# A two-filter FFT mix on one core: a read-back in halves, two row loads apart, a gate turned by four wide matmuls, and a reordered program

## The chip, the core and the metric

The kernel runs on one core of a Trainium2 chip. TensorE (PE; its weight loads are shown as PEld), VectorE (DVE), ScalarE (ACT) and GpSimd (POOL) each work through their own list of instructions in order; SyncE (SP) issues nearly all DMA transfers, also in order. The metric is device microseconds (us) for one launch; the profile gives in addition the span from the first to the last instruction of one execution.

## The reference

For x of 2048 x 1024 (bf16) the kernel computes

```
g = sigmoid((x * gate_w).sum(-1))          # one number per row of 1024
a = irfft2(rfft2(x) * (A_w_r + i A_w_i))   # filter A
b = irfft2(rfft2(x) * (B_w_r + i B_w_i))   # filter B
out = g * a + (1 - g) * b
```

with both inverse transforms rounded to bf16. B_x is not used.

## The kernel before, in words

The two-dimensional transforms are matmuls with constant tables. A row number is written s1 + 16 * s2; s2 (128 values) lies on the partitions, s1 (16 values) beside it. Columns are split by symmetry into an even ("e", 0) and an odd ("o", 1) part. The work has these stages, and each has a short name in the program's order:

- **x, W, c**: loads by SP of rows of x, of the 16 weight blocks W:0 to W:15 (512 KB each; 0 to 7 into `Ro`, 8 to 11 into `wx`, 12 to 15 into `y`), and of constants (F1, EZ, E, w0, FD, WF, PM, WJ, IG).
- **F1:s1:part:bank** (line 330): transform over s2, eight matmuls into a PSUM bank. There are eight banks, 0 to 7. **FC** copies half of the bank into one of eight temporary slots in `wx`, **FD** (DVE, line 378) forms sum and difference into `y`; or **FX** copies the whole bank and **FP** does the same on POOL.
- **F2:n:half:bank** (line 454), for 16 units n (0 to 7 even, 8 to 15 odd): transform over columns; **T** copies it out. **F3:n** (line 484) finishes the forward transform over s1; **X** copies.
- **P:n** (DVE, line 501): product with both filters, 4096 elements per partition. For the even units **Y, NA, N** mend the first column.
- **J:n** (line 547): inverse over s1, into two pairs of banks; **R:n:half:engine** (lines 200 or 202) copies each pair into a buffer `rl` (five buffers). **H:n:half** (line 559) stores it to a scratch array in DRAM; **L:part:v** (line 564) reads it back in another arrangement, eight reads v of 512 KB for each part, after all eight units of that part are stored. The even part goes into `Re`, the odd into `Ro`.
- **V:part:v:s:bank** (line 575): inverse over s2, with the gate folded into the tables EA = g * E and EB = (1 - g) * E; **VC** copies. **C** or **U** (lines 600 and 591): inverse over columns. Even results: **E**, **ES** and **EF**, or **EX** and **EQ**, leave them in `Re`. Odd results are added to and subtracted from them: **OR** and **QD** on DVE, **OC**, **OP** and **QP** for POOL. **S:S:v** stores the output.
- Gate: **gc** makes coefficients on POOL, **GH** contracts y with them on TensorE, **GC** copies to `zs`, **GT:g** turns the result by small matmuls (line 417), **GK** copies, **GZ** and **GS** make the sigmoid, **GA** and **GB** build EA and EB for four s1 at a time.

A token such as `R:15:0:A` names the operation, its unit or row, and the engine (A, D, P, S). One string `ORDER` lists all 575 tokens, written out by hand; each engine takes its own in that order, and semaphores are set where data, a PSUM bank or a buffer is shared. No planner orders anything when the kernel is built. The products that follow the odd read-back alternate with V's on TensorE, and each V must be copied out before its U or C.

Of the kernel before, what the change touches and what calls it, by code (L numbers as in the profile page):

```python
# [10 lines left out]
P = 128  # L11
# [25 lines left out]
F2:7:0:3 F2:5:1:0 Y:3:4 P:3:b Y:2:1 NA:3:D T:5:0:A T:5:1:A F3:4:6 X:4:A c:S:FD:1:2 GT:2:5 F2:7:1:2 GK:D NA:2:D N:2:D T:7:0:D
J:0:0:4 N:3:D T:7:1:A R:0:1:A R:0:0:D J:3:2:6 GZ:0:0 R:3:1:D R:3:0:A F3:5:4 GS:0 c:S:IG X:5:A F2:6:0:7 P:4:b J:2:0:2 Y:4:6
T:6:0:A R:2:1:A F2:6:1:7 NA:4:D GZ:1:5 T:6:1:A R:2:0:D N:4:D GS:1 F3:7:2 Y:5:4 X:7:A P:5:b F2:8:1:5 F3:6:6 W:S:9 NA:5:D H:1:1
H:1:0 N:5:D H:0:1 H:0:0 H:2:0 T:8:1:A H:3:1 W:S:14 J:4:2:0 W:S:15 X:6:A F2:8:0:4 R:4:0:A H:2:1 T:8:0:A F2:9:1:5 R:4:1:A H:3:0  # L40
J:5:2:6 R:5:0:A Y:7:0 P:7:b H:5:0 F2:9:0:1 Y:6:4 P:6:b F3:8:2 R:5:1:A NA:7:D NA:6:D N:7:D T:9:1:D T:9:0:D X:8:A GA:D:0 N:6:D
F2:10:1:0 F2:10:0:4 H:4:1 T:10:1:A T:10:0:A GB:D:0 P:8:b F3:9:2 X:9:A J:7:6:0 J:6:2:4 R:7:1:A F3:10:0 R:7:0:A F2:11:0:6
R:6:1:A GA:D:8 R:6:0:D H:5:1 H:4:0 H:7:1 H:7:0 H:6:0 H:6:1 W:S:13 F2:12:0:3 X:10:A F2:11:1:7 F2:12:1:0 T:11:0:A W:S:12
T:11:1:A F2:14:1:1 F3:11:6 P:9:b T:12:0:A L:0:0 J:8:4:2 T:12:1:A X:11:A T:14:1:A R:8:0:A P:10:b GA:D:4 R:8:1:D F2:13:1:0
F3:12:6 T:13:1:A F2:13:0:1 F2:14:0:0 X:12:A T:13:0:D GA:D:12 J:9:2:4 P:11:b R:9:1:D T:14:0:A L:0:2 J:10:0:6 L:0:1 R:9:0:A
L:0:6 L:0:7 L:0:4 L:0:5 V:0:0:1:2 F2:15:1:3 R:10:0:A F3:14:0 R:10:1:A VC:0:0:1:A J:11:4:6 X:14:A F2:15:0:0 R:11:1:A C:0:0:1:1
H:8:1 P:12:b H:8:0 H:9:1 H:9:0 H:10:0 H:10:1 V:0:0:0:6 R:11:0:A T:15:1:D GB:D:4 T:15:0:D P:14:b F3:13:2 V:0:1:1:7 EX:0:1:A
VC:0:0:0:A X:13:A J:12:0:4 VC:0:1:1:A R:12:1:A F3:15:2 X:15:A EQ:0:1:0:P V:0:2:1:6 R:12:0:D C:0:0:0:5 EX:0:0:A C:0:1:1:7
V:0:2:0:2 EX:1:1:A VC:0:2:0:A J:14:0:4 P:13:b VC:0:2:1:A R:14:0:A J:13:6:2 C:0:2:1:0 R:14:1:A R:13:0:A V:0:1:0:4 P:15:b
EX:2:1:D GB:D:12 EQ:2:1:0:D R:13:1:D VC:0:1:0:A C:0:2:0:5 EX:2:0:A H:12:1 H:12:0 J:15:0:6 H:11:0 H:11:1 R:15:1:A V:0:6:0:4  # L50
V:0:6:1:5 H:14:0 R:15:0:A H:14:1 C:0:1:0:3 H:13:0 H:13:1 GB:D:8 EX:1:0:A VC:0:6:0:A EQ:1:1:1:D EQ:2:0:0:D H:15:1 V:0:4:1:6
V:0:5:1:7 V:0:5:0:2 H:15:0 VC:0:6:1:D V:0:4:0:0 C:0:6:0:4 EQ:2:0:1:P EQ:1:0:1:P VC:0:5:0:D C:0:6:1:3 L:0:3 V:0:7:0:5 L:1:1
VC:0:5:1:A L:1:3 E:6:0:A L:1:6 L:1:7 C:0:5:1:7 L:1:0 EQ:0:0:1:P VC:0:4:1:A EQ:0:0:0:P C:0:5:0:1 VC:0:7:0:D V:0:7:1:2
C:0:4:1:4 ES:5:1:A VC:0:4:0:A EF:5:1 EQ:1:1:0:P EQ:0:1:1:P ES:5:0:A L:1:2 L:1:5 E:6:1:D EF:5:0 ES:4:1:D VC:0:7:1:A C:0:4:0:6
V:0:3:1:0 C:0:7:1:2 EQ:2:1:1:P EQ:1:0:0:D VC:0:3:1:A EX:7:1:A V:0:3:0:5 C:0:7:0:3 C:0:3:1:7 VC:0:3:0:A ES:4:0:A V:1:1:0:0
V:1:1:1:2 C:0:3:0:1 EX:7:0:D EF:4:1 EF:4:0 VC:1:1:0:A V:1:3:1:4 E:3:0:A U:1:1:0:3 V:1:3:0:1 E:3:1:D EQ:7:0:1:P VC:1:3:1:A
C:1:3:1:7 OC:1:0:A VC:1:1:1:D EQ:7:1:0:D VC:1:3:0:A QD:3:1:0 V:1:6:1:5 C:1:3:0:4 QD:3:0:0 U:1:1:1:2 V:1:6:0:6 VC:1:6:1:A
V:1:0:0:1 QD:3:1:1 VC:1:6:0:A EQ:7:0:0:P V:1:0:1:5 OP:1:0:1 VC:1:0:0:A QD:3:0:1 OP:1:0:0 C:1:6:1:0 OR:1:1:1 OR:1:1:0 QD:6:1:0
U:1:0:0:7 VC:1:0:1:A QP:3:0:1:P C:1:6:0:2 QD:6:0:0 V:1:5:1:1 V:1:2:1:4 U:1:0:1:3 L:1:4 QD:6:0:1 OC:0:0:A V:1:5:0:5 QD:6:1:1
VC:1:2:1:A VC:1:5:1:A QP:3:1:0:P QP:3:1:1:P QP:3:0:0:P U:1:2:1:6 VC:1:5:0:A OR:0:1:1 OP:0:0:1 OR:0:1:0 OR:2:1:0 OR:2:1:1  # L60
# [35 lines left out]
def make_constants():  # L96
# [24 lines left out]
    c["EZ"] = _bf16np(EZ.reshape(128, 128) / 128)  # L121
    j = np.arange(256) - 255.5
# [60 lines left out]
def gated_mix(ctx, tc, x_in, we_in, wo_in, w0_in, gw_in, out):  # L183
# [97 lines left out]
    def gate_coef(e):  # L281
# [3 lines left out]
        q.memset(C["one"][:], 1.0)  # L285
# [67 lines left out]

    def f1_ps(s1, par):

        if ("F1", s1, par) in PS:
            return PS["F1", s1, par].rearrange("p (a b) -> p a b", a=2)
        return PS["F1", s1, "b"].rearrange("p (a b) -> p a b", a=2)[:, :, sl(par)]
# [38 lines left out]
    def gate_hat(k):  # L397
        ps = PS["gh"] = ptile(k)
        for v in range(2):
            for e in range(2):  # L400
                for b in range(2):
                    for j in range(4):
                        nc.tensor.matmul(ps[32 * j:32 * j + 32, 0:512], lhsT=C["gwz"][:, v, e, b, :],  # L403
                                         rhs=y[:, v, e, b, 8 * j:8 * j + 8, :, :].rearrange("p t s c -> p (t s c)"),
                                         start=(v + e + b == 0), stop=(v + e + b == 3))

    def gate_copy(e):
        zs = TM["zs"] = C["EB"][:].rearrange("p a b -> p (a b)")[:, 0:512].rearrange("p (s f) -> p s f", s=NS1)
# [49 lines left out]
    def f2c(n, tt, e):  # L458
# [3 lines left out]
        cp(e, Ts[n][:, tt], PS.pop(("T", n, tt)))  # L462

# [91 lines left out]

    def scratch_store(n, tt, q="S"):
# [26 lines left out]

    def i3(par, v, s, k):
# [8 lines left out]
    def i3f(par, v, s, k):  # L593
# [3 lines left out]
        for ch in range(4):  # L597
            o = (ch // 2) * 256
            g = C["IG"][:, par, ch % 2]
            nc.tensor.matmul(ps[:, o:o + 256], lhsT=Vs[par, v][:, s, ch, :], rhs=g[:, o:o + 256], start=(ch % 2 == 0), stop=(ch % 2 == 1))  # L600

# [121 lines left out]
```

## Time and profile before

| | us |
|---|---|
| median of 3 runs | 116.35 (114.51 to 118.43) |
| profiled execution | 115.38 |
| its span | 113.6 |
| PE, DVE, ACT, POOL busy | 99.9, 97.7, 87.1, 41.0 |
| DMA | 36.79 MB, mean 324 GB/s |
| store of the last scratch half, to landing | 3.42 |
| 16 weight products on DVE (line 501) | 2.28 each |

Busy times are of the one profiled execution. A share over the whole span mixes stages, so stages are read from stretches of time. In timelines and in the chain, the columns are start, length, engine, line, operation, tiles and count; brackets hold the idle time just before and what ended it. "DMA sc<-rl" is a scratch store, "re<-sc" and "ro<-sc" are the read-backs of the even and the odd part. SPq is SP's own queue of DMA issues. Where a time of one token is given, it is the instruction of that place in its engine's list.

### The profile page before, as it was taken

Reading aid. Unit: us, or ns where it says so; the run is one execution under the profiler, and the core shown is the slowest. Engines: PE = TensorE matmul, PEld = TensorE weight load, DVE = VectorE, ACT = ScalarE, POOL = GpSimd, SP = SyncE. Lnnn points to the kernel's source line nnn. Section 1 sums busy time; section 2 is a strip of 40 time slices with the busy share of each in tenths; the row PEclk is TensorE's granted clock in tenths of the full one; section 3 lists DMA queues with packets and bytes.
Section 4 is the critical chain, followed back from the end, with each engine's and each line's share of the span. In section 5 each row is a group of like instructions: output and inputs, shape, how many; then the busy total and the mean of one; then the engine's idle time right before and its main releaser. Section 6 shows DMA issues by size and latency. Waiting matters only on the chain.

```text
span 113.6 us, 3933 instructions
## 1 busy us (share of the span) xinstructions
PE 99.9 (88%) x1616; PEld 69.7 (61%) x1619; DVE 97.7 (86%) x157; ACT 87.1 (77%) x142; POOL 41.0 (36%) x61
## 2 busy tenths in 40 slices
PE   5999979999988879798998989979999699999910
PEld 2699969776564455554654556556988477767400
DVE  0079989999998999999999999999559849999870
ACT  4267848999989999999999999999976565635200
POOL 1089999100000000000000008002590469999970
PEclk9999999999999999999999999999999999999995
DMA  3999999999999919995899999998968999445984
GB/s 85 352 325 396 398 395 406 401 404 409 400 415 391 330 68 256 292 372 208 281 298 414 414 398 349 378 388 282 309 197 338 351 408 362 190 188 226 371 326 185
DMA packets 17794, 36.79 MB, mean 324 GB/s; under 512 B 1904, under 2 KB 10736, under 8 KB 17776
## 3 DMA queue, kind: packets, MB, share of 16 engines
q1 hardware_dynamic: 17488, 36.44, 87.6%
q8 instruction: 12, 0.20, 0.7%
q10 hardware_dynamic: 288, 0.10, 0.4%
q14 instruction: 6, 0.05, 0.1%
HBM read 23.96 MB, written 12.58 MB: 322 GB/s over the span
## 4 chain that ended last, share of the span: by engine, by line
DMA 43%; PE 36%; DVE 5%; issue 4%; ACT 4%; SPq 3%; DVEq 1%; ACTq 0%
DMA sc<-rl 17%; DMA re<-in_x_dram 12%; PE ps L591 8%; PE ps L575 6%; PE ps L454 6%; DMA re<-sc 5%; DMA ro<-sc 5%; PE ps L330 4%; PE ps L547 4%; DMA y<-in_wo_dram 3%; ACT rl L200 3%; PE ps L484 3%; PE ps L600 2%; PE ps L403 2%; SPq L559 2%
## 5 line engine op out<-in xcount | busy, mean ns | idle before, releaser
L625 POOL TENSOR_TENSOR re<-wx 128x256 f32<-128x256 f32 x11 | 9.5, 888 | 60.2 <-DMA re<-sc 48.4
L200 ACT COPY wx<-ps 128x256 f32<-128x256 f32 (+1 forms) x42 | 18.3, 476 | 8.3 <-PE ps L330 5.2
L200 ACT CAST rl<-ps 128x1024 bf16<-128x1024 f32 x24 | 23.6, 1036 | 0.9 <-PE ps L547 0.5
L200 ACT CAST V<-ps 128x512 bf16<-128x512 f32 x27 | 15.7, 613 | 7.8 <-PE ps L575 5.1
L454 PE MATMUL ps<-fd,y 128*128 128x256 bf16 x128 | 17.6, 273 | 2.3 <-ACT ea L430 0.6
L501 DVE TENSOR_TENSOR p<-X,ro 128x4096 bf16<-128x4096 bf16 x8 | 18.1, 2279 | 0.0
L547 PE MATMUL ps<-p,wj 32*64 32x512 bf16 x512 | 17.1, 380 | 0.9 <-ACT V L200 0.4
L200 ACT CAST X<-ps 128x1024 bf16<-128x1024 f32 x16 | 17.0, 1060 | 0.6 <-PE ps L417 0.3
L378 DVE TENSOR_TENSOR y<-ps,wx 128x256 bf16<-128x256 f32 x48 | 16.4, 411 | 0.4 <-ACT wx L200 0.4
L330 PE MATMUL ps<-f,re 128*128 128x128 bf16 x256 | 15.2, 220 | 0.7 <-DMA re<-in_x_dram 0.7
L330 PEld LDWEIGHTS <-re 128*128 128x128 bf16 x256 | 14.7, 99 | 1.6 <-DMA re<-in_x_dram 0.9
L454 PEld LDWEIGHTS <-y 128*128 128x128 bf16 x128 | 11.4, 97 | 6.6 <-issue 5.2
L200 ACT CAST T<-ps 128x512 bf16<-128x512 f32 x26 | 15.0, 625 | 0.4 <-PE ps L484 0.2
L378 POOL TENSOR_TENSOR y<-wx 128x256 bf16<-128x256 f32 x16 | 11.1, 734 | 5.2 <-ACT wx L200 5.2
L547 PEld LDWEIGHTS <-wj 32*64 32x64 bf16 x512 | 7.6, 103 | 7.1 <-issue 3.2
L645 DVE TENSOR_TENSOR ot<-re,ps 128x512 bf16<-128x512 f32 x18 | 11.3, 682 | 0.6 <-POOL re L625 0.5
L591 PE MATMUL ps<-ig,V 128*128 128x512 bf16 x45 | 11.5, 379 | 0.2
L600 PE MATMUL ps<-ig,V 128*128 128x256 bf16 x80 | 11.2, 272 | 0.2 <-ACT rl L200 0.2
L484 PE MATMUL ps<-T,wf 64*64 64x512 bf16 (+1 forms) x128 | 10.3, 334 | 0.9 <-issue 0.3
L202 DVE CAST rl<-ps 128x1024 bf16<-128x1024 f32 x8 | 9.7, 1218 | 0.4 <-PE ps L547 0.4
L657 POOL TENSOR_TENSOR ot<-pq 128x512 bf16<-128x512 f32 x8 | 9.9, 1276 | 0.0
L575 PEld LDWEIGHTS <-ro 128*128 128x128 bf16 x128 | 7.8, 98 | 2.9 <-DMA ro<-sc 1.4
(62 smaller groups left out, 143.8 us busy)
## 6 DMA issues: line engine op xcount, KB each, us to landing
sc<-rl SPq DMA_DIRECT2D x32, 256.0 KB, 4.7
ro<-in_we_dram SPq DMA_DIRECT2D x8, 512.0 KB, 7.9
re<-sc SPq DMA_DIRECT2D x8, 512.0 KB, 7.9
ro<-sc SPq DMA_DIRECT2D x8, 512.0 KB, 6.9
re<-in_x_dram SPq DMA_DIRECT2D x7, 512.0 KB, 7.7
out_dram<-ot SPq DMA_DIRECT2D x7, 512.0 KB, 2.6
wx<-in_wo_dram SPq DMA_DIRECT2D x4, 512.0 KB, 9.6
y<-in_wo_dram SPq DMA_DIRECT2D x4, 512.0 KB, 4.9
```

The source lines that it names most:

```text
L200: nc.scalar.copy(out=out, in_=in_)
L330: nc.tensor.matmul(o, lhsT=lh, rhs=rh, start=(h == 0), stop=(h == 1))
L378: Q[e].tensor_tensor(yo[:, v, k:k + n, s1, :], a.rearrange("p (k c) -> p k c", c=4), b.rearrange("p (k c) -> p k c", c=4), op)
L454: nc.tensor.matmul(ps[:, v * 256:v * 256 + 256], lhsT=y[:, v, par, b, 2 * t:2 * t + 2, :, :].rearrange("p j s c -> p (j s c)"), rhs=C["FD" ...
L484: nc.tensor.matmul(view(ps[ho, tt * 512:(tt + 1) * 512], dst), lhsT=lh, rhs=view(T[hp(jh), tt, :], src), start=(w == 0), stop=(w == 1))
L501: nc.vector.tensor_tensor(p[:], xb, wb, ALU.mult)
L547: nc.tensor.matmul(o, lhsT=lh, rhs=src[r, ri, wi, tt], start=(q == 0), stop=(q == 3))
L575: nc.tensor.matmul(ps[:, ch * 128:ch * 128 + 128], lhsT=RR[par][:, v, ch // 2, s, c0 + 256 * ab:c0 + 256 * ab + 128], rhs=Ew[:, s1, :], st ...
L591: nc.tensor.matmul(ps, lhsT=Vs[par, v][:, s, ch, :], rhs=rh, start=(ch == 0), stop=(ch == 3))
L600: nc.tensor.matmul(ps[:, o:o + 256], lhsT=Vs[par, v][:, s, ch, :], rhs=g[:, o:o + 256], start=(ch % 2 == 0), stop=(ch % 2 == 1))
L645: nc.vector.tensor_tensor(otile(v)[:, s, h, :], EV[:, v, s], PS["O", 1, v, s], (ALU.add, ALU.subtract)[h])
L657: Q[e].tensor_tensor(otile(v)[:, :, h, 256 * g:256 * g + 256], t[:, :, 0], t[:, :, 1], (ALU.add, ALU.subtract)[g])
```

## The change

Five things change.

- The load of rows 2 and 3 of x becomes two loads.
- The read-back L:1:1 (the first of the odd part) becomes L:1:1:0 and L:1:1:1, each with the rows of one s.
- GT (four tokens, 64 matmuls of one column) becomes one token Gt of four matmuls with 128 rows, 128 columns of weights and four columns of data. For it GH reads y in another order of the same elements, GC writes `zs` in another arrangement, and gc sets a mask of four columns by five memsets instead of one.
- Tokens change places. On SP, w0 and E go behind x:14, WJ:0:4 and PM come earlier, FD:1:2 and WJ:4:16 too; the order of the weights becomes 1, 2, 0, 3, 5, 7, 11, 4, 10, 8, 6, 9, 15, 12, 14, 13 (before 0, 2, 1, 5, 3, 7, 6, 10, 4, 8, 11, 9, 14, 15, 13, 12); H:8:0 goes ahead of L:0:0, H:2:0 behind H:5:0. Many PSUM banks are renumbered.
- Copies change engines. To ScalarE: FC:1:e, T:15:0, VC:0:6:1, VC:0:5:0, VC:0:7:0, VC:1:1:1, VC:1:4:1, ES:4:1, EX:7:0. To VectorE: FC:3:e, VC:0:1:1, R:15:0, EX:1:0, E:6:0, VC:0:4:1, EX:7:1, OC:1:0, EQ:1:1:0, EQ:2:0:1. To POOL: EQ:2:1:0.

The diff also adds helper functions for pairs and halves that no token calls, and a constant ID that is not loaded; they are left out here.

```diff
-warm:8 c:A:F1 x:S:0:1 x:S:1:1 c:A:gws x:S:2:2 F1:0:o:1 F1:1:o:4 F1:0:e:2 FC:0:e:D F1:1:e:3 tab:A FX:0:o:A FX:1:o:A x:S:4:2
-x:S:6:2 x:S:8:2 F1:3:e:6 F1:2:e:1 FP:0:o c:S:EZ x:S:10:2 FC:3:e:A c:S:w0 c:S:E x:S:12:2 x:S:14:2 gc:P FP:1:o FC:1:e:D FD:1:e
+warm:8 c:A:F1 x:S:0:1 x:S:1:1 c:A:gws x:S:2:1 x:S:3:1 tab:A F1:0:o:6 FX:0:o:A x:S:4:2 F1:0:e:0 F1:1:e:4 F1:1:o:1 FC:1:e:A
+FC:0:e:D FD:0:e FD:1:e F1:2:e:5 F1:2:o:6 F1:3:o:4 x:S:6:2 FX:1:o:A F1:3:e:1 FC:2:e:A FX:2:o:A x:S:8:2 F1:5:e:6 FX:3:o:A
+FP:0:o FP:1:o FP:2:o FP:3:o x:S:10:2 FD:2:e c:S:EZ x:S:12:2 x:S:14:2 FC:3:e:D c:S:WF:0:4 c:S:FD:0:1 c:S:w0 F1:4:e:2 F1:4:o:4
...
-V:0:6:1:5 H:14:0 R:15:0:A H:14:1 C:0:1:0:3 H:13:0 H:13:1 GB:D:8 EX:1:0:A VC:0:6:0:A EQ:1:1:1:D EQ:2:0:0:D H:15:1 V:0:4:1:6
-V:0:5:1:7 V:0:5:0:2 H:15:0 VC:0:6:1:D V:0:4:0:0 C:0:6:0:4 EQ:2:0:1:P EQ:1:0:1:P VC:0:5:0:D C:0:6:1:3 L:0:3 V:0:7:0:5 L:1:1
+R:15:1:A VC:0:6:1:A VC:0:6:0:A V:0:5:0:6 EQ:0:0:1:P R:15:0:D EQ:1:1:0:D H:11:0 C:0:6:1:2 H:14:0 H:14:1 H:13:0 H:13:1 H:15:1
+V:0:4:0:0 H:15:0 EQ:1:1:1:D VC:0:5:0:A L:0:3 L:1:1:0 C:0:6:0:1 L:1:1:1 L:1:3 EX:1:0:D L:1:0 L:1:6 EQ:0:0:0:P V:0:5:1:6
...
-V:0:3:1:0 C:0:7:1:2 EQ:2:1:1:P EQ:1:0:0:D VC:0:3:1:A EX:7:1:A V:0:3:0:5 C:0:7:0:3 C:0:3:1:7 VC:0:3:0:A ES:4:0:A V:1:1:0:0
-V:1:1:1:2 C:0:3:0:1 EX:7:0:D EF:4:1 EF:4:0 VC:1:1:0:A V:1:3:1:4 E:3:0:A U:1:1:0:3 V:1:3:0:1 E:3:1:D EQ:7:0:1:P VC:1:3:1:A
+V:0:3:1:2 EQ:7:1:0:D ES:4:1:A VC:0:3:1:A C:0:7:0:1 EQ:1:0:1:P V:0:3:0:0 EX:7:0:A VC:0:3:0:A C:0:3:1:2 L:1:2 V:1:1:0:5
+V:1:1:1:7 VC:1:1:0:A C:0:3:0:3 VC:1:1:1:A U:1:1:0:6 V:1:3:1:5 V:1:3:0:7 E:3:1:D E:3:0:A VC:1:3:1:A EQ:1:0:0:D OC:1:0:D
+VC:1:3:0:A V:1:0:0:2 EQ:7:0:1:P C:1:3:1:3 EF:4:1 QD:3:1:1 QD:3:1:0 U:1:1:1:1 C:1:3:0:4 QD:3:0:1 QD:3:0:0 EQ:7:0:0:P V:1:6:1:7
+V:1:6:0:5 V:1:0:1:3 EQ:7:1:1:P V:1:2:1:6 VC:1:6:1:A OP:1:0:0 C:1:6:1:4 OP:1:0:1 QP:3:1:1:P VC:1:6:0:A OR:1:1:1 OR:1:1:0
...
@@ gate_coef
-        q.memset(C["one"][:], 1.0)
+            q.memset(C["mk"][:], 0.0)
+            for j in range(4):
+                q.memset(C["mk"][32 * j:32 * j + 1, j:j + 1], 1.0)
@@ gate_hat
-    rhs=y[:, v, e, b, 8 * j:8 * j + 8, :, :].rearrange("p t s c -> p (t s c)"),
+    rhs=y[:, v, e, b, :, 4 * j:4 * j + 4, :].rearrange("p t s c -> p t (s c)")
@@ new
+    def gate_turn_all(k):
+        ps = PS["gt"] = ptile(k)
+        o = ps[:, 0:NS1].rearrange("p (j s) -> p s j", j=4)
+        for s in range(4):
+            nc.tensor.matmul(o[:, s], lhsT=TM["zs"][:, s, :], rhs=C["mk"][:], start=True, stop=True)
@@ scratch_load(par, v, s="b", q="S")
+        if s != "b":
+            s = int(s)
+            i = SC[par][:].rearrange("a (h v r s) m -> (a h) v s r m", h=4, v=8, r=2)
+            Q[q].dma_start(o.rearrange("p (r s m) -> p s r m", r=2, s=2)[:, s], i[:, v, s])
+            return
```

## The prediction

> **What bounds the kernel now.** I read the page (shares, slices, chain), then busy times by stage, then the chain in order of time, then timelines at the joints. The shares (PE 88%, DVE 86%, ACT 77%, DMA about 88%) name no bound; the stages do. Columns: stretch and its length, busy time of each engine, clock, DMA share, GB/s.
>
> ```profile
> 6.00:24.00 18.00, 17.26 (x284) 15.81 (x281) 17.33 (x51) 14.18 (x35) 14.01 (x31) 1.00 1.02 390
> 24.00:38.00 14.00, 13.05 (x306) 8.05 (x294) 13.61 (x19) 13.17 (x19) 0.00 (x0) 1.00 1.03 402
> 38.00:62.00 24.00, 21.09 (x409) 12.44 (x417) 23.80 (x27) 23.58 (x33) 0.00 (x0) 1.00 0.83 272
> 62.00:77.00 15.00, 13.42 (x272) 8.61 (x256) 15.00 (x13) 14.98 (x21) 2.50 (x1) 1.00 1.05 386
> 77.00:88.00 11.00, 10.98 (x167) 9.28 (x165) 8.34 (x18) 8.97 (x18) 5.10 (x8) 1.00 0.84 278
> 88.00:104.00 16.00, 14.97 (x157) 10.78 (x158) 13.85 (x26) 8.40 (x15) 13.22 (x12) 1.00 0.77 300
> ```
>
> See that from 38 to 77 us VectorE (third busy time) and ScalarE (fourth) both work without a pause, 38.8 and 38.6 of 39 us, and that from 77 us TensorE (first) does: 10.98 of 11, then 14.97 of 16. So two joints matter: when the last inverse unit (J:15) can start, and what TensorE waits for after it.
>
> The chain (start, length, what) shows the second joint, the scratch round trip:
>
> ```profile
> 66.73 8.73 DMA sc<-rl
> ...
> 79.21 1.03 ACT rl L200
> 80.24 0.02 issue
> 80.25 3.42 DMA sc<-rl
> ...
> 84.26 5.43 DMA ro<-sc
> 89.69 0.05 issue
> 89.74 0.62 PE ps L575 x8
> ```
>
> Two copies of J:15's result run one behind the other on ScalarE (R:15:1 78.30 to 79.31, R:15:0 79.21 to 80.23), the store H:15:0 leaves at 80.25 and lands at 83.67, then the odd read-backs are issued, the first (L:1:1) 83.88 to 84.21, landing at 87.32; the next (L:1:3) lands at 89.69. The timeline of TensorE shows what that costs:
>
> ```profile
> 88.27 0.60 PE L600 MATMUL ps<-ig,V 128*128 128x256 bf16 x4
> 89.74 0.23 PE L575 MATMUL ps<-ea,ro 128*128 128x128 bf16 x1 [0.87 <-DMA ro<-sc]
> ```
>
> V:1:1:0 itself started at 87.36, with no pause: TensorE got there just as L:1:1 landed. The pause of 0.87 us is for L:1:3. At the end VectorE is late:
>
> ```profile
> 107.55 2.48 DVE L645 TENSOR_TENSOR ot<-re,ps 128x512 bf16<-128x512 f32 x4 [0.46 <-POOL re L625]
> ```
>
> Four output sums follow the last-but-one product U:1:7:1 (ends 107.44); the last store S:4 leaves at 110.09 and lands at 112.70. The profiled execution took 115.38 us, 1.78 more than its span of 113.6; I count against 115.38. The median of the runs is 116.35, from 114.51 to 118.43, so a change under about 2% can't be told from none here.
>
> **Start (rows x2, x3 apart; F1 reordered).** FC:0:e moves up one product (0.45 us), so VectorE starts at 5.79 instead of 6.24. Walking the new order with the rows' durations (F1 0.445 us apart, FD 0.67, FC 0.37 on ScalarE, 0.42 on VectorE, FX 0.59): FC:0 5.79 to 6.21, FD:0 to 6.97, FD:1 to 7.63, FD:2 to 8.3. But F1:3:o now writes bank 4, which FD:1:e reads until 7.63; F1:3:e behind it ends at 8.7, so FC:3:e, now on VectorE, waits 0.4 us, and FD:3:e ends at 9.93 (before: 9.88). The early start is given back. Later, w0 and E (96 KB) no longer stand before x12: at 400 GB/s that is 0.24 us, so x12 lands near 14.8 instead of 15.05; F1:5:o now follows it (+0.45). F2:1:0 starts near 19.75 (19.21), F3:1 near 22.2 (22.08), and P:1, behind VectorE, at 24.4 as before. Sum: 0, bounds -0.45 and +0.5. ScalarE needs F3:1 only by 22.8.
>
> **Gate.** 64 one-column products go (0.6 us of chain, 0.42 + 0.19) and four wide ones come. No row has their shape; the 128x2 products with PM last 165 ns and follow 25 ns apart, F1's 128x128 ones 56 ns, so four take 0.1 to 0.3 us. Gain on TensorE 0.3 to 0.5, not on the path at 31 us, where P products on VectorE set the pace. Four more POOL memsets, 0.09 each, hide: POOL idles from 20 to 68. GH now reads y in runs of 16 with gaps. No such row: 1.9 us for 32 as it stands from below, double from above. I take it as free, nearest to the strided F3 rows (399 ns for 512 columns, GH 380). Doubled, X:3 would come 1.9 us late against P:3's slack of about 1.7 (X:3 ends 30.39; P:3, now behind GK, NA:2, N:0 and NA:3, starts near 32.1): +0.2. Those four small operations before P:3 take nothing out of the sum; they start J:0 0.2 us sooner and so most of the 0.35 us VectorE waits at R:0:0 goes: -0.2.
>
> **Middle, 38 to 77.** ScalarE gets T:15:0 (0.6), gives VC:0:1:1 (0.6): its gapless run to R:13:0 (77.05) is unchanged. VectorE changes the same two and takes one more GB before P:15 (0.41): P:15 ends near 76.2 less the 0.2 above, 76.0. J:15 needs R:13:0's banks: 77.1 as now. Bounds: -1.0, if the new order also closes ScalarE's own pauses from 24 to 62 us (0.22, 0.14, 0.33, 0.28 and small ones, 1.2 together), +0.5 if pauses come. T:15:0 on ScalarE is read by F3:15 near 69.5, whose X:15 ends about 72.2 against P:15 at 73.7: hidden.
>
> **SP queue.** Each DMA uses one of eight semaphores in turn and is issued only when the one eight before has landed: store H:9:0 leaves at 66.73, read-back L:0:1, eight before, landed at 66.67. H:8:0 now stands before L:0:0, which so waits for R:8:0: 58.15 + 1.1 us, issue near 59.6 instead of 58.22. But W:12 (512 KB, landing 61.22, just ahead of L:0:0 at 62.49) went forward to the idle stretch at 43 us. L:0:0 lands near 62.7, the seven even reads follow 1.27 us apart, and H:8:1 lands within 1 us before its 73.43; R:14:0, which reuses that buffer, starts at 74.21. Cost 0, bounds -0.7 and +1.4. W:9, 15, 14 come early enough (P:9 at 54 us).
>
> **Last unit and read-back.** R:15:0 on VectorE: P:15 76.0, EX:2:1 0.6, GB 0.4, R:13:1 1.2, R:15:0 1.2 gives 79.5, beside R:15:1 on ScalarE to 79.3. H:15:0 leaves near 79.6, 0.65 earlier. It lands 2.3 us later on 15 of the 16 engines now and 3.4 on the last: 82.0 to 83.0, so the odd reads start 0.7 to 1.7 us earlier; I take 0.9. The halves read 1 KB rows where the whole read 4 KB; the packets show 46 ns per KB stored against 159 ns for 4 KB, so the pair costs 2 x 256 x 46 / 16 = 1.47 us for 1.27, plus one issue of 0.45: L:1:3 gains 0.9 - 0.3 = 0.6 and lands at 89.1.
>
> TensorE from J:15 to V:1:1:0 has the same 20 operations, so V:1:1:0 stays near 87.25: the half lands before it, but the whole would too. Its worth lies in U:1:1:0, now placed ahead of V:1:3:1 (0.86 us into the 0.87 us pause). V:1:3:1 starts at 89.45 with U:1:1:0 done: 1.15 us won. Then V:1:0:0 comes third and needs L:1:0: 89.1 + 1.4 = 90.5, against 90.35: 0.1 lost. And V:1:0:1 now writes bank 3, held by C:1:3:1 until QD:3:0:1; that stands behind QD:3:1:0, which needs C:1:3:0. From V:1:0:0: products 2.4, then two QD 1.3 gives +3.7; TensorE would be there at +3.1: 0.6 lost. What remains is 20 operations without a wait: U:1:7:1 ends about 0.5 earlier.
>
> **End.** VC:1:4:1 (0.68) leaves VectorE and EQ:7:1:1 stands early on POOL, so the four sums follow U:1:7:1 at once: 0.1 more. POOL's fourteen operations at 1.26 us from about 90 end near 108.5 (109.93). S:4 near 109.5. **Sum: -0.6 us, 114.8.**
>
> The page "DMA: Bandwidth & Descriptors" of the Trainium skill, section "Bandwidth", speaks against the halves: batch to 1 MiB, small transfers are mostly fixed cost. By the fit in its section "Anatomy of one DMA" (2.0 us plus bytes over 436 GB/s) I estimate 2.6 us for a half and 3.2 for the whole. The trace has 3.1 for the whole and, with the queue full, 0.65 us per 256 KB store: fixed parts overlap, against the rule.
>
> **Rivals.** Forecast, 114.8: 0.56.
> Faster, 0.22: ScalarE's pauses of 1.2 us close, so J:15 comes at 76, and QD:3 doesn't hold bank 3 (0.6): -2.4, 113.0. For: ScalarE is the bound up to 77. Against: the pauses are waits for products whose order hardly changes.
> Slower, 0.12: H:8:0 holds the even reads. If L:0:0 lands 1.4 us later, H:8:1 lands near 74.8, and R:14:0, at 74.21, waits for it; it decides as soon as L:0:0 is more than 0.8 late (H:8:1 lands at 73.43 now). That is up to 1.4 on J:15. H:15:0, behind a queue as full as the one H:14:0 met (75.25 to 80.27, 5.0 us instead of 3.4), brings 1.5 more at V:1:3:1: +2.9 on the forecast, 117.7. For: eight semaphores make every store wait for a read. Against: W:12's 1.27 us are gone from that queue.
> Slower by serial landing, 0.04: if each half took a whole landing as L:1:1's, 3.1 us, one after the other, L:1:3 would land 2.1 later than forecast, near 91.2, and L:1:0 with it: +2.1, 116.9. Against: the last five odd reads land 1.27 us apart. The page named above would have it so.
> The split does nothing, 0.06: L:1:3 is the one that matters and gains nothing from an earlier store, so it lands 0.3 later than now, at 90.0, and L:1:0 at 91.4 instead of 90.5: +0.9, 115.7.
>
> The ends give 113.0 and 117.7. Faster by over 2% 0.22, within 0.60, slower 0.18, part of that for banks I didn't walk.
>
> **What would show it.** Right: no pause at 89 us, R:15:0 and R:15:1 side by side, H:15:0 leaving before 80, a wait of about 0.6 before V:1:0:1, P:1 at 24.4. Wrong: VectorE or ScalarE with pauses between 38 and 77, L:0:0 landing after 64, J:15 away from 77 by more than 0.7.

## The result, and the profile after

The changed kernel takes 116.4 us (median of 4 runs, 116.1 to 116.63). The ratio to the kernel before, which leaves out executions more than 1.5% above the fastest of their kernel, is 1.014, with a 95% interval of 1.009 to 1.019: some 1.6 us slower, where 0.6 us faster was forecast. The time lies inside the range, on the wrong side. The profiled execution after took 116.63 us with a span of 114.8 (before: 115.38 and 113.6), so the pair of traces holds 1.25 us to be explained.

Busy times by stretch of the kernel after; columns as in the prediction: stretch and length, PE, PEld, DVE, ACT, POOL, clock, DMA share, GB/s.

```profile
38.00:62.00 24.00, 21.36 (x408) 12.73 (x415) 23.97 (x27) 23.62 (x33) 0.00 (x0) 1.00 0.90 299
62.00:77.00 15.00, 13.08 (x272) 8.23 (x256) 14.86 (x12) 14.95 (x20) 3.11 (x2) 1.00 1.02 356
77.00:88.00 11.00, 11.00 (x170) 9.75 (x168) 10.37 (x21) 8.90 (x19) 4.37 (x7) 1.00 0.89 299
88.00:104.00 16.00, 13.84 (x142) 9.76 (x142) 11.98 (x21) 7.41 (x15) 12.14 (x11) 1.00 0.78 286
```

Up to 88 us nothing is lost: VectorE and ScalarE work almost without a pause to 77 (38.83 and 38.57 of 39 us), TensorE without one from 77 to 88, and J:15 starts at 77.14 (77.16 before). Only the last row costs time: TensorE was busy for 14.97 of its 16 us before and is for 13.84 now, 1.13 us less. The timeline of TensorE after (start, length, engine, line, operation; L703 is U, L675 is V; the bracket is the idle time just before) shows where:

```profile
88.57 1.04 PE L703 MATMUL ps<-ig,V 128*128 128x512 bf16 x3
...
91.28 0.23 PE L675 MATMUL ps<-ea,ro 128*128 128x128 bf16 x1 [1.67 <-DMA ro<-sc]
...
92.73 0.23 PE L675 MATMUL ps<-ea,ro 128*128 128x128 bf16 x1 [0.39 <-DMA ro<-sc]
```

U:1:1:0 runs where it was meant to, at 88.57, right behind V:1:1:1. Then comes a pause of 1.67 us before V:1:3:1, nearly twice the 0.87 that it was to fill, and another of 0.39 before V:1:0:0. Both end with a landing of an odd read-back: L:1:3 at 91.23 (89.69 before) and L:1:0 at 92.68. The chain after (start, length, what) gives the way there:

```profile
59.77 3.08 DMA re<-sc
...
79.81 4.36 DMA sc<-rl
...
85.72 6.96 DMA ro<-sc
92.73 0.62 PE ps L675 x8
```

The last odd store, H:15:0, leaves at 79.81, 0.44 us earlier than before, and takes 4.36 us instead of 3.42: it lands at 84.16, 0.49 *later*. The odd reads then take 7.07 us from that landing to L:1:3's, instead of 6.02. At the other end VectorE's four sums (L826) follow TensorE as before, 1.13 us later:

```profile
108.68 2.48 DVE L826 TENSOR_TENSOR ot<-re,ps 128x512 bf16<-128x512 f32 x4 [0.39 <-PE ps L703]
```

From V:1:6:1 on, which follows those two, TensorE keeps one rhythm: U:1:7:1 starts 12.7 us after it here (94.92 and 107.61), and in every variant of the changed kernel below. What V:1:3:1 and V:1:0:0 lose reaches the end whole.

### The profile page after: what moved, and what is told of

Same layout as the page of the kernel before. It is cut to its first block, busy times and chain, and to the rows that moved or that the text cites. A ratio compares the mean times of both kernels' runs of the same rounds, so it can differ in the third digit from the quotient of the medians.

```text
span 114.8 us, 3821 instructions
## 1 busy us (share of the span) xinstructions
PE 99.2 (86%) x1556; PEld 69.6 (61%) x1559; DVE 98.3 (86%) x157; ACT 87.1 (76%) x143; POOL 41.1 (36%) x64
## 4 chain that ended last, share of the span: by engine, by line
PE 35%; DMA 25%; ACT 17%; DVE 8%; issue 7%; SPq 3%; DVEq 1%; ACTq 0%
PE ps L336 9%; PE ps L703 8%; ACT rl L201 8%; DMA sc<-rl 7%; DMA re<-in_x_dram 6%; PE ps L675 6%; DMA ro<-sc 6%; DVE p L586 5%; PE ps L528 4%; ACT T L201 4%; ACT X L201 4%; DMA wx<-in_wo_dram 3%; PE ps L632 3%; DMA re<-sc 3%; PE ps L712 2%
## 5 line engine op out<-in xcount | busy, mean ns | idle before, releaser
L806 POOL TENSOR_TENSOR re<-wx 128x256 f32<-128x256 f32 x10 | 9.0, 924 | 59.4 <-ACT wx L201 51.8
L201 ACT COPY wx<-ps 128x256 f32<-128x256 f32 (+1 forms) x41 | 17.5, 460 | 9.0 <-PE ps L336 5.3
L201 ACT CAST V<-ps 128x512 bf16<-128x512 f32 x30 | 16.6, 602 | 9.6 <-PE ps L675 7.0
L201 ACT CAST rl<-ps 128x1024 bf16<-128x1024 f32 x23 | 23.1, 1048 | 0.7 <-PE ps L632 0.6
L528 PE MATMUL ps<-fd,y 128*128 128x256 bf16 x128 | 17.0, 273 | 1.5 <-DVE zt L203 0.8
L826 DVE TENSOR_TENSOR ot<-re,ps 128x512 bf16<-128x512 f32 x18 | 11.2, 682 | 1.3 <-issue 0.9
L703 PE MATMUL ps<-ig,V 128*128 128x512 bf16 x45 | 11.5, 379 | 0.2
L203 DVE CAST rl<-ps 128x1024 bf16<-128x1024 f32 x9 | 10.9, 1217 | 0.2 <-PE ps L632 0.2
L675 PEld LDWEIGHTS <-ro 128*128 128x128 bf16 x128 | 7.7, 98 | 4.0 <-DMA ro<-sc 2.7
```

The source lines that it names most:

```text
L201: nc.scalar.copy(out=out, in_=in_)
L203: Q[e].tensor_copy(out=out, in_=in_)
L528: nc.tensor.matmul(ps[:, v * 256:v * 256 + 256], lhsT=y[:, v, par, b, 2 * t:2 * t + 2, :, :].rearrange("p j s c -> p (j s c)"), rhs=C["FD" ...
L675: nc.tensor.matmul(ps[:, ch * 128:ch * 128 + 128], lhsT=RR[par][:, v, ch // 2, s, c0 + 256 * ab:c0 + 256 * ab + 128], rhs=Ew[:, s1, :], st ...
L703: nc.tensor.matmul(ps, lhsT=Vs[par, v][:, s, ch, :], rhs=rh, start=(ch == 0), stop=(ch == 3))
L826: nc.vector.tensor_tensor(otile(v)[:, s, h, :], EV[:, v, s], PS["O", 1, v, s], (ALU.add, ALU.subtract)[h])
```

## The experiments

Two causes are in question. **Theory A**: the two halves of L:1:1 hold up the read behind them. **Theory B**: the odd stores end late because H:8:0, ahead of L:0:0 in SP's queue, made the even reads leave late. Ratios are to the kernel before, timed beside each group, since chips and hours differ. For later use, the landings from the trace's sixteen landing events per transfer (one for each DMA engine), in us. The ratio is of several executions of a kernel, the landings are of the one that was profiled:

| kernel | ratio [95%] | L:0:0 | H:15:0 | last of L:1:1 | L:1:3, first to last engine | H:15:0 to L:1:3 |
|---|---|---|---|---|---|---|
| before | 1 | 62.49 | 83.67 | 87.32 | 88.24 to 89.69 | 6.02 |
| after | 1.014 [1.009, 1.019] | 63.87 | 84.16 | 87.62 | 88.52 to 91.23 | 7.07 |
| after, again (c_after) | 1.014 [1.007, 1.020] | 64.03 | 84.05 | 87.94 | 88.68 to 91.39 | 7.34 |
| after, whole (e1) | 0.999 [0.995, 1.002] | 63.47 | 84.10 | 87.82 | 88.61 to 89.08 | 4.98 |
| after, H:8:0 back (e4) | 1.002 [0.998, 1.006] | 63.15 | 83.35 | 87.43 | 87.71 to 90.75 | 7.40 |
| after, both (e5) | 0.990 [0.985, 0.995] | 62.99 | 82.89 | 86.50 | 87.27 to 87.78 | 4.89 |
| both, W:13 early (e6) | 0.991 [0.987, 0.996] | 62.85 | 83.16 | 87.00 | 87.61 to 88.24 | 5.08 |
| after, R:15:0 on ScalarE (e7) | 1.015 [1.008, 1.021] | 64.09 | 84.33 | 87.87 | 88.83 to 92.15 | 7.82 |
| after, halves of 4 KB rows (e8) | 1.002 [0.997, 1.007] | 63.97 | 84.17 | 88.16 | 88.56 to 89.27 | 5.10 |
| after, L:1:6 first (e11) | 1.042 [1.033, 1.052] | 63.30 | 83.72 | 87.07 | 88.47 to 91.56 | 7.84 |
| before, halves (e2, again) | 1.004 [0.999, 1.009] | 63.29 | 83.10 | 87.14 | 87.81 to 89.10 | 6.00 |
| before, halves, L:1:0 first (e12) | 1.010 [1.006, 1.015] | 63.12 | 83.46 | 87.55 | 88.32 to 89.77 | 6.31 |
| before, U:1:1:0 first (e3) | 1.006 [1.002, 1.010] | 64.35 | 83.84 | 87.75 | 89.03 to 89.78 | 5.94 |
| before, H:8:0 first (e10) | 1.011 [1.002, 1.019] | 66.10 | 85.25 | 89.43 | 89.76 to 90.67 | 5.42 |
| after, L:1:3 in halves too (e9) | 1.006 [1.002, 1.010] | 63.10 | 82.76 | 86.99 | 86.46 to 89.63 | 6.87 |

### The read whole again (e1)

```diff
-V:0:4:0:0 H:15:0 EQ:1:1:1:D VC:0:5:0:A L:0:3 L:1:1:0 C:0:6:0:1 L:1:1:1 L:1:3 EX:1:0:D
+V:0:4:0:0 H:15:0 EQ:1:1:1:D VC:0:5:0:A L:0:3 L:1:1 C:0:6:0:1 L:1:3 EX:1:0:D
```

> The changed kernel with L:1:1 read in one piece again. Theory A, the halves: their 1 KB rows and the extra issue are what makes L:1:3 land at 91.2 (forecast 89.1), so in one piece L:1:3 lands by 89.9, the pause before V:1:3:1 falls from 1.7 to under 0.6 us, and the kernel is 1.0 us faster than the changed one (about 115.4, within 0.5% of before). Theory B, the late even reads: the halves do nothing, L:1:3 stays near 91 and the time within 0.3 us of the changed kernel's 116.4.

114.83 us, and the loss is gone. TensorE in this kernel:

```profile
87.87 0.23 PE L675 MATMUL ps<-ea,ro 128*128 128x128 bf16 x1 [0.24 <-DMA ro<-sc]
...
88.77 0.60 PE L712 MATMUL ps<-ig,V 128*128 128x256 bf16 x4
89.22 1.04 PE L703 MATMUL ps<-ig,V 128*128 128x512 bf16 x4
```

There is no bracket behind U:1:1:0 any more. V:1:1:0 waits 0.24 us for the whole read, and V:1:3:1 follows U:1:1:0 without a wait for data at 90.10. H:15:0 landed at 84.10, as late as in the changed kernel, yet L:1:3 landed at 89.08, 1.26 us behind L:1:1 and not 3.6. Theory A holds, at more than its expected size.

### The halves alone, and U:1:1:0 alone, in the kernel before (e2, e3)

```diff
-VC:0:5:0:D C:0:6:1:3 L:0:3 V:0:7:0:5 L:1:1 VC:0:5:1:A L:1:3
+VC:0:5:0:D C:0:6:1:3 L:0:3 V:0:7:0:5 L:1:1:0 L:1:1:1 VC:0:5:1:A L:1:3
```
```diff
-VC:1:1:0:A V:1:3:1:4 E:3:0:A U:1:1:0:3 V:1:3:0:1
+VC:1:1:0:A U:1:1:0:3 V:1:3:1:4 E:3:0:A V:1:3:0:1
```

> The kernel before with nothing changed but L:1:1 read in two halves. Theory A: L:1:3 lands about 1.5 us later than 89.7 and the kernel is 1.0 us slower than before, ratio near 1.009. Theory B: ratio within 0.3% of 1, L:1:3 at most 0.3 us later, as the packets' 46 ns per KB give.

> The kernel before with U:1:1:0 moved ahead of V:1:3:1 and nothing else. By the prediction's step this fills the pause of 0.87 us; C:1:3:1 then waits for its copy until about 91.0 instead of 91.5, so 0.45 us faster, ratio 0.996. If the odd reads that follow are late as in the changed kernel by their nature, nothing is gained, ratio 1.

Halves alone: 115.65 us, ratio 0.999 [0.994, 1.005], where Theory A had 1.009 (the medians of all executions, 115.65 and 114.99, give 1.006). In its trace L:1:3 lands 1.41 us behind the second half, so the halves didn't delay it there. U:1:1:0 alone: 115.57 us, 1.006 [1.002, 1.010]: 0.2 to 1.0% slower, where 0.4% faster was expected. The trace doesn't say why. In it the move does what it should: V:1:3:1 starts at 90.12 behind U:1:1:0 without a pause. But that execution was 0.5 us behind at P:1, long ahead of the edit, and 0.9 at J:15 (78.05), so its end can't be compared.

The profiled execution of the first was its fastest by 1.2 us, so the same kernel was run once more:

> The kernel before with L:1:1 in halves, once more: its profiled execution in the first group was, at 114.04, 1.2 us faster than the next of ten (115.28 to 116.12), so its trace isn't typical. If halves cost the read behind them in this order too, an execution near the median of 115.6 has L:1:3 landing 2.5 to 4.3 us after the second half. If the order of the kernel before is immune to it, 1.3 to 1.6 again.

115.48 us, 1.004 [0.999, 1.009]; L:1:3 1.96 us behind the second half, 6.00 from H:15:0's landing, as in the kernel before with the whole read (6.02). In that program halves cost between nothing and 0.9%.

### H:8:0 back behind the even reads (e4), and both edits (e5)

```diff
-F2:13:0:1 F2:14:0:0 J:9:2:4 T:13:0:D X:12:A T:14:0:A P:11:b H:8:0 L:0:0 J:10:0:6 L:0:1
+F2:13:0:1 F2:14:0:0 J:9:2:4 T:13:0:D X:12:A T:14:0:A P:11:b L:0:0 J:10:0:6 L:0:1
...
-F3:13:2 L:0:6 V:0:0:0:7 T:15:0:A EQ:0:1:1:P T:15:1:D VC:0:1:1:D J:12:0:4 X:13:A L:0:2 L:0:7 L:0:4 L:0:5 H:8:1
+F3:13:2 L:0:6 V:0:0:0:7 T:15:0:A EQ:0:1:1:P T:15:1:D VC:0:1:1:D J:12:0:4 X:13:A L:0:2 L:0:7 L:0:4 L:0:5 H:8:0 H:8:1
```

> The changed kernel with store H:8:0 back behind the even reads, ahead of H:8:1. Theory B: L:0:0 leaves 1.4 us earlier (58.3 for 59.77), the even reads end earlier, H:15:0 lands 0.5 to 1.2 us before 84.16, and the kernel is 0.5 to 1.2 us faster than the changed one. Theory A: H:15:0 may land earlier, but L:1:3 still follows the halves by 3.6 us and the time is within 0.3 us of the changed one's.

115.33 us, 1.002: about 1.2% of the loss goes, so Theory B holds as well. L:0:0 leaves at 59.00 instead of 59.77, less than the 1.4 expected, since it now waits for the landing of H:6:0 (58.86), whose semaphore it reuses. It lands 0.7 earlier, and H:15:0 with it (83.35 against 84.16). The halves are still there, and so is the wait behind them:

```profile
90.80 0.23 PE L675 MATMUL ps<-ea,ro 128*128 128x128 bf16 x1 [1.40 <-DMA ro<-sc]
```

Now both, with the changed kernel itself beside it:

> The changed kernel again, unchanged, so that the others of this group have it beside them. Both theories: ratio to the kernel before 1.007 to 1.017, L:1:3 landing near 91 us, the sums OR:4:1:1 ending near 111. If it is within 0.3% of the kernel before, the loss of the first comparison was the state of that chip, and neither theory (the halves; the late even reads) is needed.

> The changed kernel with L:1:1 whole again and H:8:0 back ahead of H:8:1, both edits of the first group together. Theory A (the halves hold L:1:3 up, by about 2 us): this is the whole-read version of the first group, 114.8, with nothing to add, L:1:3 near 89. Theory B (the odd stores end late because the even reads left late): this is the version with H:8:0 back, 115.3. Both at work, each by its own amount: L:0:0 leaves near 59.0, H:15:0 lands 0.5 to 1.0 earlier than in the changed kernel, L:1:3 near 88.3, 114.2.

The changed kernel gave 116.59, 1.014 [1.007, 1.020], with L:1:3 at 91.39: the loss repeats. With both edits the time is 113.85 us, ratio 0.990 [0.985, 0.995]: **faster than both kernels**. The two effects add, within their intervals: 1.5% for the whole read (1.014 to 0.999), 1.2% for H:8:0 (1.014 to 1.002), 2.4% for both. Busy times by stretch of this kernel:

```profile
77.00:88.00 11.00, 11.00 (x172) 9.92 (x172) 10.50 (x21) 9.13 (x19) 4.65 (x7) 1.00 0.92 313
88.00:104.00 16.00, 16.00 (x168) 11.45 (x166) 14.09 (x24) 9.05 (x18) 14.54 (x13) 1.00 0.73 293
```

TensorE is busy for 27.00 of 27.00 us. L:1:3 lands at 87.78, V:1:3:1 starts at 88.99 behind U:1:1:0, L:1:0 lands at 89.20 for V:1:0:0 at 89.88. The read-back is hidden: no product waits for a landing there any more.

### Is it the bytes in the queue? W:13 early (e6)

```diff
+N:6:D H:3:1 W:S:9 GA:D:4 W:S:15 W:S:12 W:S:14 W:S:13 P:8:b X:9:A J:6:2:4
...
-H:7:0 H:6:0 J:8:4:2 P:10:b W:S:13 T:12:1:A X:11:A
+H:7:0 H:6:0 J:8:4:2 P:10:b T:12:1:A X:11:A
```

(On top of e5.)

> The version before this one in the group, with the last weight block W:13 (512 KB) loaded right behind W:14, at about 45 us, instead of just ahead of the even reads. Theory B: those 512 KB take 1.27 us of the DMA engines; if the even reads, and behind them the odd stores, are late because of the queue, all of them come up to 1.27 us earlier: L:0:0 lands near 62, H:8:1 near 73, H:15:0 at 82 to 83, L:1:3 near 88, 113.5 to 114.2. Theory A: the same as the version before it, within 0.3%.

114.29 us, 0.991, no different from e5. L:0:0's own flight shortened by 1.1 us (3.60 from issue to last engine, 4.69 in e5), but it left 0.95 us later, because H:6:0, whose semaphore it takes, landed at 59.11 instead of 58.16. What the flight gained, the issue lost, and H:15:0 landed at 83.16 (82.89 in e5). So this run doesn't tell what an earlier start of the even reads is worth.

### Does the copy set the store's end? R:15:0 back on ScalarE (e7)

```diff
-R:15:1:A VC:0:6:1:A VC:0:6:0:A V:0:5:0:6 EQ:0:0:1:P R:15:0:D EQ:1:1:0:D H:11:0
+R:15:1:A VC:0:6:1:A VC:0:6:0:A V:0:5:0:6 EQ:0:0:1:P R:15:0:A EQ:1:1:0:D H:11:0
```

> The changed kernel with R:15:0 back on ScalarE, behind R:15:1. The prediction gave that move 0.65 us at the store's issue and 0.9 at its landing. If the end of H:15:0 is set by the transfers queued ahead of it, it lands at 84.0 to 84.4 here too and the time is that of the changed kernel within 0.3%. If it is set by when the copy ends, H:15:0 lands 0.65 to 0.9 later, near 84.9, and the time grows by 0.4 to 0.7.

116.52 us, 1.015: the time of the changed kernel. Behind R:15:1 and two V copies, ScalarE ended R:15:0 at 81.97, 2.1 us later than VectorE did in the changed kernel run beside it (79.88). The chains of the changed kernel, run again, and of this one:

```profile
80.33 3.73 DMA sc<-rl
...
85.61 7.04 DMA ro<-sc
```
```profile
82.00 2.33 DMA sc<-rl
...
85.89 7.58 DMA ro<-sc
```

A store that leaves 1.67 us later lands 0.28 later (84.33 against 84.05). So in the changed kernel the end of the copy doesn't set the landing: R:15:0 on VectorE won an issue, and some 1.4 us of it bought no landing. That it is the stores queued ahead is the reading that fits; in e7 itself the flight of 2.33 us is the shortest of all traces here (2.36 to 4.36 in the others), so there the late copy may just have caught up with the queue.

### Rows or loads? Halves with 4 KB rows (e8)

```diff
-            i = SC[par][:].rearrange("a (h v r s) m -> (a h) v s r m", h=4, v=8, r=2)
-            Q[q].dma_start(o.rearrange("p (r s m) -> p s r m", r=2, s=2)[:, s], i[:, v, s])
+            i = SC[par][:].rearrange("a (h v q) m -> (a h) v (q m)", h=4, v=8)
+            Q[q].dma_start(o[64 * s:64 * s + 64], i[64 * s:64 * s + 64, v])
```

> The changed kernel with L:1:1 still in two loads, but each with half of the partitions, so that every row of a load stays 4 KB; V:1:1:0 needs both. If the 1 KB rows are what holds up the read behind them (in the changed kernel L:1:3 lands 3.3 to 4.3 us after the second half, behind the whole L:1:1 only 1.3), L:1:3 lands 1.2 to 1.6 us after the second half, near 89.3, and the time is that of the whole-read version, 114.8 to 115.3. If it is the number of loads or the issue in between, L:1:3 lands 3 us or more behind the second half and the time is 116.5.

115.41 us, 1.002 [0.997, 1.007]: the time of the whole read, not of the halves, though there are as many loads and issues as in the changed kernel. L:1:3 lands 1.11 us behind the second half. The chain of this kernel goes through the second half into V:1:1:0 (which needs both) and then on along TensorE:

```profile
84.25 3.91 DMA ro<-sc
88.21 1.07 PE ps L675 x16
```

So it is the shape of the halves, rows of 1 KB, and not their number or their size. (With the row length e8 also changes which partitions a half fills; no run separates these two.) The last columns of the table say how: in the changed program, behind 4 KB rows the sixteen engines finish L:1:3 within 0.5 to 0.7 us of each other, behind 1 KB rows within 2.7 to 3.3, while the *first* engine ends at the same distance from the store (4.4 to 4.6 us from H:15:0's landing in both runs of the changed kernel, in e1 and in e8). It is not one late engine either: the mean of the sixteen landings of L:1:3 is 89.60 in the changed kernel and 88.75 in e1. A matmul waits for the last.

### One step or many? L:1:3 in halves too (e9)

```diff
-L:0:3 L:1:1:0 C:0:6:0:1 L:1:1:1 L:1:3 EX:1:0:D L:1:0
+L:0:3 L:1:1:0 C:0:6:0:1 L:1:1:1 L:1:3:0 L:1:3:1 EX:1:0:D L:1:0
```

> The changed kernel with L:1:3 in two halves of 1 KB rows as well. If what costs is the step from 1 KB rows to 4 KB rows, the halves of L:1:3 follow those of L:1:1 at 0.7 us each and land by 89.3, and the slow start moves to L:1:0, which lands 3 to 4 us later, near 92.7 as in the changed kernel: V:1:3:1 at 89.3, the time 115.8 to 116.6. If every half read costs its own, the halves of L:1:3 land at 91 or later, L:1:0 at 93 or later, and the time is 116.8 or more.

115.66 us, 1.006 [1.002, 1.010], better than either theory had it. The halves of L:1:3 landed 1.32 and 2.64 us behind those of L:1:1, not 0.7 and 1.4, and L:1:0 only 1.30 after them, not 3 to 4. The waits of TensorE:

```profile
89.67 0.23 PE L675 MATMUL ps<-ea,ro 128*128 128x128 bf16 x1 [0.72 <-DMA ro<-sc]
...
90.97 0.23 PE L675 MATMUL ps<-ea,ro 128*128 128x128 bf16 x1 [0.23 <-DMA ro<-sc]
```

Neither "a slow start at the step from 1 KB to 4 KB" nor "each half costs its own" fits. The trace is of an early execution: H:15:0 landed at 82.76 here, and from that landing L:1:3 took 6.87 us, little less than in the changed kernel. The ratio is of ten executions and doesn't rest on this one; why it is better than that of the changed kernel stays open.

### H:8:0 ahead, alone, in the kernel before (e10)

```diff
-P:9:b T:12:0:A L:0:0 J:8:4:2 T:12:1:A X:11:A T:14:1:A R:8:0:A P:10:b
+P:9:b T:12:0:A J:8:4:2 T:12:1:A X:11:A T:14:1:A R:8:0:A H:8:0 L:0:0 P:10:b
...
-H:8:1 P:12:b H:8:0 H:9:1
+H:8:1 P:12:b H:9:1
```

> The kernel before with the one edit of SP's queue alone: H:8:0, and L:0:0 behind it, right after R:8:0. If the transfers from the first even read to the last odd store run as one full queue (20 to 21 us from L:0:0's landing to H:15:0's in all runs so far), L:0:0 lands 1.0 to 1.4 us later, H:15:0 0.5 to 1.2 later, V:1:3:1 with it, and the ratio to the kernel before is 1.004 to 1.011. If the queue has slack, as the prediction had it (cost 0), the ratio is within 0.3% of 1.

116.74 us, 1.011 [1.002, 1.019], at the upper end of what was expected, but not only by the queue. In the kernel before, V:0:0:1 stands where L:0:0 lands, and TensorE waits there:

```profile
66.14 0.23 PE L575 MATMUL ps<-ea,re 128*128 128x128 bf16 x1 [2.56 <-DMA re<-sc]
```

L:0:0 landed at 66.10, 3.6 us later than in the kernel before and not 1.0 to 1.4. J:15 came at 79.80 (77.16 in the kernel before; 0.8 of the difference was there at P:1 already), R:15:0 ended at 82.86, and H:15:0 left at 82.89 and landed at 85.25, 1.6 later than in the kernel before. With a flight of 2.36 us it was late because its copy was, so this run doesn't test the full queue: the time went by way of V:0:0:1 and J:15. The edit costs time in either program; which wait passes it on depends on what stands behind the read.

### Is it the read order? (e11, e12)

In the order of the kernel before, halves spread L:1:3 over 1.3 us; in the changed one over 2.7. The read behind L:1:3 differs (L:1:6 there, L:1:0 here), so each program got the other's order (the second pair of lines is the kernel before with halves):

```diff
-L:1:3 EX:1:0:D L:1:0 L:1:6 EQ:0:0:0:P
+L:1:3 EX:1:0:D L:1:6 L:1:0 EQ:0:0:0:P
```
```diff
-VC:0:5:1:A L:1:3 E:6:0:A L:1:6 L:1:7 C:0:5:1:7 L:1:0 EQ:0:0:1:P
+VC:0:5:1:A L:1:3 E:6:0:A L:1:0 L:1:6 L:1:7 C:0:5:1:7 EQ:0:0:1:P
```

> The changed kernel, halves and all, with L:1:6 ahead of L:1:0 as in the kernel before. If it is which read follows L:1:3 that matters, L:1:3 lands 1.4 to 2.4 us after the second half, with its 16 engines landing within 1.3 us of each other (2.7 in the changed kernel). If the order has no part in it, L:1:3 lands 3.3 us or more after, with 2.2 us or more between its engines. In both cases L:1:0 lands later by up to 1.8 us and V:1:0:0 waits for it, so the time is 116 to 118.

> The kernel before with halves and with L:1:0 ahead of L:1:6, the read order of the changed kernel. If the order matters, L:1:3 lands 3 us or more after the second half, its engines 2 us apart or more, and the time is 117 or more. If not, 1.4 to 2.0 us after and 1.3 apart, as with the halves alone; L:1:6 then lands about 1.3 later, V:1:6:1 waits for it, and the time is 115.8 to 117.

120.21 us (1.042) and 115.91 us (1.010). In the first, L:1:3 lands 4.5 us behind the second half with 3.1 between its engines, so the order isn't the cause; and as L:1:0 lands later, V:1:0:0 waits again, and the time is far above what was expected (the last line is a row of stretch and busy times):

```profile
91.61 0.23 PE L675 MATMUL ps<-ea,ro 128*128 128x128 bf16 x1 [2.03 <-DMA ro<-sc]
...
94.10 0.29 PE L675 MATMUL ps<-ea,ro 128*128 128x128 bf16 x1 [1.43 <-DMA ro<-sc]
94.18 0.31 PE L675 MATMUL ps<-eb,ro 128*128 128x128 bf16 x1
...
93.00:97.00 4.00, 2.90 (x16) 1.95 (x17) 0.92 (x2) 0.39 (x1) 0.00 (x0) 0.57 1.00 400
```

Its profiled execution is 2.66 us longer than the changed kernel's. The waits are half of that: V:1:0:0 starts 1.4 us later (94.10 and 92.73). The other half is TensorE's clock. From 93 to 97 us the granted clock is 0.57 (0.50 from 94 to 96), and the products of V follow 0.11 us apart instead of 0.056; from V:1:0:0 to V:1:6:1 it takes 3.50 us where the changed kernel took 2.19. In all other traces here it is 0.97 or more in every microsecond from 56 to 109 us. It fell behind two pauses of 2.03 and 1.43 us; a single one of 2.56 us (e10) and those of the changed kernel (1.67 and 0.39) did not do it, and what does is not shown.

In the second it lands 2.2 us behind, 1.45 between its engines; with the halves alone it was 1.4 and 2.0, 0.6 and 1.3. In the kernel before the whole read already spread L:1:3 over 1.45 (0.75 in e3 and 0.91 in e10, where it is whole too), so the traces show no more spread by halves there. Why 4 KB rows run closer together in the changed program, and 1 KB rows further apart, stays open.

## Why the prediction was wrong

**Start: small slips, rightly worth nothing.** FC:3:e waited 0.97 us and not 0.4, because F1:3:o came at 8.43, behind the last engine of row 3 (8.38), and FD:3:e ended at 10.75 (forecast 9.93). F2:1:0 at 20.08 (19.75) and P:1 at 24.84 (24.4) are late, and the lag is gone at R:0:0, 35.26 (35.32 before).

**Gate: right.** GH took 1.91 us with the gaps in y and 1.91 without, and the four wide products 0.24 us (estimate 0.1 to 0.3).

**Middle: right.** J:15 at 77.14, forecast 77.1; P:15 ended at 76.48 instead of 76.0 and still came in time.

**SP queue: the first term that was mis-sized.** "L:0:0 lands near 62.7", and then "Cost 0, bounds -0.7 and +1.4". It left at 59.77, close to the 59.6 forecast, and landed at 63.87; H:8:1 landed at 73.96, not before 73.43. J:15 did not suffer, as forecast (R:14:0 at 74.06), so the cost looked like nothing at the place where I looked for it. With H:8:0 back, H:15:0 landed at 82.89 to 83.35 (e4, e5, e6); with it ahead, at 83.72 to 84.33 in six of seven traces of the changed order (82.76 in e9, where L:0:0 had landed early too, at 63.10). In all of these H:15:0 lands 19.7 to 20.6 us after L:0:0, even where the copy ends 2.1 us later (e7). I read this as one full conveyor from the first even read to the last odd store, on which a late start is a late end. It is a reading of this program only: in the kernel before and its variants the distance is 19.2 to 21.2, and e3, with L:0:0 1.9 us later than the kernel before, has H:15:0 only 0.2 later. Undoing the edit is shown to be worth 1.2%; that all of it passes through the queue is read from the landings, and neither e6, which was to move the start alone and did not, nor e10 tests it.

**Last unit: failed with it.** "H:15:0 leaves near 79.6, 0.65 earlier", and would land "82.0 to 83.0, so the odd reads start 0.7 to 1.7 us earlier; I take 0.9". (The terms ahead of it add to 79.4, not 79.5; that is small.) It left at 79.81 and landed at 84.16, 0.49 later than before. I took the flight of the old store, 2.3 to 3.4 us, as a property of the store; in the changed kernel an earlier issue only made it longer (3.73 us, and 2.33 in e7, which left 1.67 later). The slower rival had this in half a sentence ("behind a queue as full as the one H:14:0 met").

**Halves: the second term that was mis-sized, and the larger.** "1.47 us for 1.27, plus one issue of 0.45: L:1:3 gains 0.9 - 0.3 = 0.6 and lands at 89.1". (0.2 and 0.45 make 0.65; the sum took 0.3 of it, and the text doesn't say why.) The halves themselves behaved: they landed 0.73 apart. What I left out is the read behind them. L:1:3 landed at 91.23, and the 2.1 us between divide into 1.4 for the store (84.16 instead of 83.67 - 0.9) and 0.7 for the reads (7.07 instead of 6.02 + 0.3). The runs size the second one higher: with 4 KB rows the new order needs only 4.9 to 5.1 us, so the 1 KB rows cost 2.1 us and more where the sum had 0.3. The packet times behind it, 46 against 159 ns, could not show it: they are the usual (median) times, and the usual packet says nothing of the last of sixteen engines.

**V and U: half right.** V:1:1:0 came at 87.22 (87.25), the half was worth nothing there, and U:1:1:0 filled the old pause; the new pause was longer. The step on bank 3 was wrong: V:1:0:1 started at 95.81 without a stall, because the middle number of QD is s: QD:3:1:1 and QD:3:1:0 both read C:1:3:1 alone, and bank 3 was free at 95.16, before QD:3:0:1 ran. I counted 0.6 us that were not there.

**End: right.** The four sums followed U:1:7:1 by 0.04 us and ended 2.52 us after it (2.59 before).

**The rivals.** The time came nearest to "slower by serial landing" (116.9, L:1:3 at 91.2), but not by its mechanism: the halves landed 0.73 us apart, not 3.1. "H:8:0 holds the even reads" was the right place for half the loss, through the store and not through J:15. Without the two mis-sized edits the rest of the change gives 0.990, about 1.2 us less than before: twice the forecast of 0.6.

On the rule that the prediction weighed against the halves: e8 moves the same two times 256 KB without loss, so it was not the size of the transfer. The page "DMA: Bandwidth & Descriptors" of the Trainium skill has, under "Specifications", line rate from 512 B up; here sixteen engines on 1 KB packets of 46 ns make 356 GB/s, on 4 KB packets of 159 ns 412, and the trouble came in the packets behind them. The rule and the fit that the prediction took from that page were measured on DMAs issued by GpSimd; here SP issues them. Its section "Rules for kernel authors" says that two transfers to disjoint halves of the partitions serialize and aren't worth it; e8 agrees, as it gains nothing over e1.

## What to carry to other kernels

Price an edit of a full queue of transfers at its far end too, and not only at the next consumer: here the next consumer lost nothing and the kernel lost 1.2%. A store's flight in a trace can include the queue ahead of it, so an earlier issue need not be an earlier landing. A load may be split for an earlier first piece, but try it with its rows kept long, and look at the spread of the engines in the loads *behind* it: the same halves of short rows cost 1.5% in one program order and 0 to 0.9% in the other.

## What was not expected of the hardware

A load is done when the last of its sixteen DMA engines is. The Trainium skill, "DMA: Bandwidth & Descriptors", section "Why a DMA increments its semaphore by 16 and not by 1", says that they finish independently and only the full count means landed; the sixteen landing events of the trace agree. What was new is how far apart they can be. The first engine ended L:1:3 at 88.52 us in the changed kernel and at 88.61 with the whole read; the last ended at 91.23 and at 89.08. Between 87 and 90 us the mean 4 KB packet of the changed kernel took 215 to 268 ns, single ones up to 1.74 us, where the median is 159. With the read whole (e1) the mean was 162 to 177 there, in the kernel before 182 to 187, and with both edits undone every 4 KB packet from 87 to 88 took 159. Stretched packets are not only found behind halves: from 45 to 60 us the mean of the changed kernel is 182. What a stretched packet waits for, the trace doesn't show, and no run here settled it.
